# A long convolution in 32-token blocks with stacked lag blocks, inside a fused attention and state-space kernel

## The chip, the cores and the metric

The kernel runs on one core of one Trainium2 chip. The metric is the device time of one execution in microseconds. Before the change it is 539.16 us (median of 4 runs, 536.37 to 542.76). The profile of a kernel is one such execution, recorded by the hardware profiler; its span is about 1.7 us shorter than the time.

In the profile lines, PE is TensorE's matmuls, PEld its loads of the stationary operand, ACT is ScalarE, DVE is VectorE. L867 is a line of the kernel.

## The reference, cut to what matters

```python
x = A_x                                   # 1 x 2048 x 448, bf16
g = sigmoid((x * gate_w).sum(-1, keepdims=True))
a = multi_query_attention(x, wq, wk, wv, wo)   # 16 heads of 28, one K and one V
# S4 layer: a causal convolution over 2048 tokens, one filter of length 2048 per channel
K = real(sum_n C[d,n] * exp(dt[d]*A[d,n]*l) * dt[d]*B[d,n])      # l = 0 .. 2047
b = causal_conv(x, K) + x * Dskip
return g * a + (1 - g) * b
```

There are thus three loads: attention (410 large exponentials on ScalarE, score and PV products on TensorE), the making of the filters K (VectorE and TensorE), and the convolution of 448 channels with 448 different filters, done as Toeplitz products on TensorE. A planner in the kernel puts the pieces in a fixed order on every engine.

## The kernel before

The convolution treats a chunk of 16 channels at a time. For one channel the 2048 tokens are 32 blocks of 64. The Toeplitz data T of a channel is the *moving* operand and the tokens U are the *stationary* one, with as many columns as there are blocks for which the lag matters. Four channels lie interleaved (8 bytes apart in T) and use four column tiles of 32.

```python
for m in range(1, 16, 2):
    def mm(e, k=k, m=m, s=s, gi=gi):
        for j in range(4):                                   # four channels, four column tiles
            r = e.matmul(ps.v(32 * j, 33 - m, po + 128 * k, [[1, 128]]),
                         self.U.v(0, P, (m - 1) * D + 4 * gi + j, [[D, 33 - m]]),                # 32..18 columns
                         self.T.v(0, P, s * 4096 + (960 - 64 * m) * 4 + j, [[4, 128]]),          # 128 columns
                         start=(m == 1), stop=(m == 15), tile_position=(0, 32 * j), skip_group_check=True)
    pg.op("pe", mm, 112, ..., mode="c32")
pg.op("dve", lambda e: e.tensor_tensor(cst..., ps..., omq..., ALU.mult), el(512), ...)     # times 1 - g
self.ytr(c)                                   # 16 transposes back to token rows, then O += on VectorE
# ... cut ...
self.skip()      # 16 times on VectorE: x * Dskip * (1 - g), and O += it
```

Here `v(p0, n, offset, [[stride, count]])` is a view of n partitions; strides are in elements, so `[[D, 33 - m]]` with D = 448 reads stationary columns 896 bytes apart.

Attention is interleaved with this. A score step fills two or three PSUM banks with 512 columns each (`tile_position=(32*h, 0)`, row tiles), ScalarE takes the exponential of them in one activation of 1,024 or 1,536 columns, and a PV step has four matmuls of 512 columns on four column tiles of 32. The score of step b + 2 is issued while step b is in ScalarE.

## Time and profile before

| | before |
|---|---|
| time, median of 4 runs | 539.16 us |
| TensorE busy, mean granted clock | 484.8 us (90%), 0.921 |
| VectorE busy | 483.9 us (90%) |
| ScalarE busy | 487.5 us (91%) |
| DMA queue of the loads, share of 16 engines | 73.7% |
| exponentials | 410, idle 18.9 us before them in all |

The prediction below shows and reads the main lines. Three more views are needed for the comparison. The first is the page's chain of work that ended last, by engine; the second the groups of TensorE with shapes kept apart (busy us, mean ns of one, then the engine's idle time before and what ended it); the third a stretch of the timeline of TensorE (start, length of the row, engine, line, shape of the first instruction of the row, how many).

```profile
PE 47%; ACT 36%; DVE 12%; DMA 2%; issue 1%; POOL 1%; DVEq 0%; POOLq 0%
```

```profile
L967 PE MATMUL psS<-qT,kT 29*128 29x512 bf16 x1024 | 170.6, 412 | 29.6 <-ACT expT L977 27.2
L985 PE MATMUL psB<-expT,vaug 128*32 128x512 bf16 x1024 | 108.8, 417 | 1.4 <-ACT gtok L643 1.3
```

### The profile page before, as it was taken

How to read it: one execution, taken by the hardware profiler on the slowest of the kernel's cores; microseconds unless marked ns; L12 is line 12 of the kernel's file. 1: busy time of each engine (PE TensorE's matmuls, PEld its weight loads, DVE VectorE, ACT ScalarE, POOL GpSimd, SP SyncE). 2: the span in 40 equal slices, each digit the busy share in tenths (PEclk: the TensorE clock that was granted, in tenths of full speed). 3: DMA queues.
4: the chain of work that ended last, by engine and by line, in shares of the span. 5: the costliest groups of instructions: out<-in, count | busy, mean ns of one | idle time of the engine just before them, and what ended most of it. 6: DMA issues, size and time to landing. Idle time of an engine off the chain costs nothing.

```text
span 537.2 us, 18418 instructions
## 1 busy us (share of the span) xinstructions
PE 484.8 (90%) x8229; PEld 243.8 (45%) x8229; DVE 483.9 (90%) x1168; ACT 487.5 (91%) x428; POOL 4.9 (1%) x17
## 2 busy tenths in 40 slices
PE   6778888999999899999999999999999998998893
PEld 5411132553545444554545445554455543544452
DVE  4978899998999999999999999999999999999023
ACT  4599998998999999999999999999999999999960
POOL 3000000000000000000000000000000000000000
PEclk9855566997999999999999999999999999889997
DMA  8735445777798867779898896778877796697954
GB/s 232 145 79 137 138 139 207 245 285 299 249 327 297 303 230 237 253 265 345 304 337 320 262 332 238 242 260 319 309 296 267 285 393 220 176 388 254 350 188 137
DMA packets 42266, 138.16 MB, mean 257 GB/s; under 512 B 8168, under 2 KB 24476, under 8 KB 27852
## 3 DMA queue, kind: packets, MB, share of 16 engines
q1 hardware_dynamic: 40396, 135.71, 73.7%
q10 hardware_dynamic: 1792, 1.29, 0.8%
q8 instruction: 64, 1.05, 0.8%
q14 instruction: 14, 0.11, 0.1%
HBM read 133.01 MB, written 3.85 MB: 255 GB/s over the span
## 4 chain that ended last, share of the span: by engine, by line
PE 47%; ACT 36%; DVE 12%; DMA 2%; issue 1%; POOL 1%; DVEq 0%; POOLq 0%
ACT expT L977 35%; PE psS L967 13%; PE psS L853 12%; PE psB L985 8%; PE psX L792 6%; PE psX L676 2%; DMA T<-KP_scratch 2%; DVE tab L767 2%; DVE tmp L762 2%; DVE tab L759 2%; PE psS L504 1%; PE psX L877 1%; PE psX L831 1%; DVE O L883 1%; DVE tab L776 1%
## 5 line engine op out<-in xcount | busy, mean ns | idle before, releaser
L977 ACT ACTIVATE expT<-psS 128x1536 bf16<-128x1536 f32 (+1 forms) x410 | 470.8, 1254 | 19.0 <-PE psB L985 12.9
L967 PE MATMUL psS<-qT,kT 29*128 29x512 bf16 x1024 | 170.6, 412 | 29.6 <-ACT expT L977 27.2
L853 PE MATMUL psS<-T,U 128*26 128x128 bf16 (+7 forms) x3584 | 157.9, 303 | 0.6 <-DMA T<-KP_scratch 0.5
L853 PEld LDWEIGHTS psS<-T,U 128*26 128x26 bf16 (+7 forms) x3584 | 113.9, 152 | 35.3 <-issue 28.2
L985 PE MATMUL psB<-expT,vaug 128*32 128x512 bf16 x1024 | 108.8, 417 | 1.4 <-ACT gtok L643 1.3
L967 PEld LDWEIGHTS psS<-qT,kT 29*128 29x128 bf16 x1024 | 39.6, 92 | 124.4 <-ACT expT L977 92.8
L762 DVE TENSOR_TENSOR tmp<-tab,mbf 128x2048 bf16<-128x2048 bf16 (+4 forms) x140 | 78.0, 563 | 0.0
L759 DVE TENSOR_TENSOR tab<-tab,mbf 128x2048 bf16<-128x2048 bf16 (+4 forms) x140 | 77.9, 563 | 0.0
L767 DVE TENSOR_TENSOR tab<-tab,tmp 128x2048 bf16<-128x2048 bf16 (+4 forms) x140 | 77.8, 563 | 0.0
L792 PE MATMUL psX<-tab 128*32 128x96 bf16 x1792 | 54.8, 268 | 1.3 <-issue 1.2
L985 PEld LDWEIGHTS psB<-expT,vaug 128*32 128x32 bf16 x1024 | 26.6, 95 | 64.2 <-issue 60.8
L792 PEld LDWEIGHTS psX<-tab 128*32 128x32 bf16 x1792 | 41.2, 116 | 14.2 <-issue 9.0
L776 DVE TENSOR_TENSOR tab<-tab,mbf 128x2048 bf16<-128x2048 bf16 x28 | 34.0, 1216 | 0.0
L778 DVE TENSOR_TENSOR tab<-tab,mbf 128x2048 bf16<-128x2048 bf16 x28 | 34.0, 1213 | 0.0
L861 DVE TENSOR_TENSOR cst<-psS,omq 128x512 bf16<-128x512 f32 x28 | 19.0, 680 | 15.7 <-PE psS L853 15.5
L717 DVE TENSOR_TENSOR msq<-mst 128x256 f32<-128x256 f32 x63 | 26.2, 416 | 0.0
L676 PE MATMUL psX<-xT,Wq 112*128 112x512 bf16 x64 | 21.7, 436 | 0.4 <-DVE O L838 0.2
L727 DVE CAST mbf<-mst 128x256 bf16<-128x256 f32 x70 | 20.1, 288 | 0.1
L720 DVE TENSOR_TENSOR mst<-msq 128x128 f32<-128x128 f32 x70 | 19.7, 282 | 0.0
L723 DVE SCALAR_TENSOR_TENSOR mst<-mst 128x128 f32<-128x128 f32 x63 | 17.8, 283 | 0.0
L804 DVE TENSOR_REDUCE kstg<-psX 128x128 bf16<-128x256 f32 x28 | 11.7, 418 | 4.2 <-PE psX L792 4.1
L730 DVE TENSOR_SCALAR mbf<-mst 128x128 bf16<-128x128 f32 x70 | 15.3, 218 | 0.0
(112 smaller groups left out, 255.8 us busy)
## 6 DMA issues: line engine op xcount, KB each, us to landing
T<-KP_scratch SPq DMA_DIRECT2D x112, 1024.0 KB, 7.8
rdenB<-R_scratch SPq DMA_DIRECT2D x60, 64.0 KB, 3.8
U<-in_A_x_dram SPq DMA_DIRECT2D x3, 896.0 KB, 5.4
tab<-in_A_x_dram SPq DMA_DIRECT2D x4, 448.0 KB, 6.9
O<-Z_scratch SPq DMA_DIRECT2D x1, 1792.0 KB, 13.6
KP_scratch<-kstg SPq DMA_DIRECT2D x28, 64.0 KB
xT<-in_A_x_dram SPq DMA_DIRECT2D x1, 1792.0 KB, 9.2
U<-Z_scratch SPq DMA_DIRECT2D x1, 896.0 KB, 8.0
```

Of the source, the lines that this page charges most:

```text
L676: pg.op("pe", lambda e, T=T: e.matmul(px, self.Wq.v(0, DT, T * 512 + g * 128, [[1, 128]]), self.xT.v(0, DT, T * S + 512 * qc, [[1, 512]]), ...
L717: pg.op("dve", lambda e, k=k: e.tensor_tensor(msq.v(0, P, 0, [[1, 2 * BW]]) if k > 1 else msq.v(0, P, 0, [[BW, 2], [1, BW]]), src_both(k - ...
L759: pg.op("dve", lambda e, d=dst, a=src, ra=ra, w=w: e.tensor_tensor(d, a, mbf.v(0, P, ra, [[8, 16], [0, 2 * w], [1, 4]]), ALU.mult), el(n, ...
L762: pg.op("dve", lambda e, a=src, rb=rb, w=w: e.tensor_tensor(tmp.v(0, P, so, [[4 * w, 32], [1, 4 * w]]), a, mbf.v(0, P, rb, [[4, 32], [0, w ...
L767: pg.op("dve", lambda e, d=dst, t=t2: e.tensor_tensor(d, d, t, ALU.add), el(n, 1.92), rd=[("tmp", s), ("tab", s, lv + 1)], wr=[("tab", s, ...
L776: pg.op("dve", lambda e: e.tensor_tensor(ua, src, mbf.v(0, P, ra, [[8, 8], [0, 64], [1, 4]]), ALU.mult), el(2048, 1.92), rd=rk + mk, wr=[( ...
L778: pg.op("dve", lambda e: e.tensor_tensor(ub, src, mbf.v(0, P, rb, [[4, 16], [0, 32], [1, 4]]), ALU.mult), el(2048, 1.92), rd=rk + mk, wr=[ ...
L792: r = e.matmul(self.psX.v(32 * g, 32, 96 * jj, [[1, 96]]), tab.v(0, P, o + 768, [[4, 32]]), tab.v(0, P, o, [[256, 3], [4, 32]]), start=(co ...
L853: r = e.matmul(ps.v(32 * j, 33 - m, po + 128 * k, [[1, 128]]), self.U.v(0, P, (m - 1) * D + 4 * gi + j, [[D, 33 - m]]), self.T.v(0, P, s * ...
L967: r = e.matmul(self.psS.v(0, P, 1536 * s + 512 * k, [[1, 512]]), kT.v(32 * h, DH + 1, 128 * kt, [[1, 128]]), qT.v(32 * h, DH + 1, 512 * qs ...
L977: pg.op("act", lambda e: e.activation(expT.v(0, P, 512 * (i0 % 10), [[1, n]]), self.psS.v(0, P, 1536 * s, [[1, n]]), AF.Exp, scale=SQ), 75 ...
L985: r = e.matmul(self.psB.v(32 * h, 32, 0, [[1, 512]]), vaug.v(0, P, 32 * kt, [[1, 32]]), expT.v(0, P, 512 * ((4 * st + h) % 10), [[1, 512]] ...
```

## The change

The intent is to halve the Toeplitz data and to do away with work that only rearranges. Tokens are cut into blocks of 32. The filter's lags are stacked so that the 128 rows of a matmul carry four adjacent lag blocks; one loaded filter image of 128 x 2,176 elements (32 columns of 68) serves two accumulations. A channel takes 16 steps m, and causality lets step m use only 64 - 4m stationary columns. Two channels (224 apart) run on two column tiles of 64. The output has tokens reversed inside a block, so the back-transposes disappear; x is stored flipped, and the output is flipped once by a product with an anti-diagonal matrix. The skip term becomes one more matmul per channel, with a small image TD that has Dskip on its diagonal, so that one accumulation, of two channels, has 34 matmuls. U becomes a ring of two slots, loaded in runs of 56 elements. The core of the diff, cut:

```diff
-KPW = 2112
+KR = 68
+KPW = 256 * KR
@@ T load (1 MB becomes 0.54 MB)
-        pg.dma([(self.T.v(0, P, s * 4096, [[1, 4096]]),
-                 dram(self.KP, 4 * gi * KPW, [[4, 64], [4096, 2], [1, 4096]]))],
+        pg.dma([(self.T.v(0, P, s * self.TW, [[1, self.TW]]), dram(self.KP, gi * KPW, [[KR, 128], [1, self.TW]]))],
@@ convolution
-            for m in range(1, 16, 2):
-                    for j in range(4):
-                        r = e.matmul(ps.v(32 * j, 33 - m, po + 128 * k, [[1, 128]]),
-                                     self.U.v(0, P, (m - 1) * D + 4 * gi + j, [[D, 33 - m]]),
-                                     self.T.v(0, P, s * 4096 + (960 - 64 * m) * 4 + j, [[4, 128]]),
-                                     start=(m == 1), stop=(m == 15), tile_position=(0, 32 * j), skip_group_check=True)
+                        for m in range(4 * mg, 4 * mg + 4):
+                            for par in range(2):
+                                r = e.matmul(ps.v(64 * par, 64 - 4 * m, po + 32 * pr, [[1, 32]]),
+                                             self.U.v(0, P, uo + 4 * m * 112 + par * 56 + e0 + pr, [[112, 64 - 4 * m]]),
+                                             self.T.v(0, P, s * self.TW + 4 * m + 2 * k1 + par, [[KR, 32]]),
+                                             start=(m == 0), stop=(m == 15), tile_position=(0, 64 * par), skip_group_check=True)
+                            if m == 0:
+                                for par in range(2):
+                                    r = e.matmul(ps.v(64 * par, 64, po + 32 * pr, [[1, 32]]),
+                                                 self.U.v(0, P, uo + par * 56 + e0 + pr, [[112, 64]]),
+                                                 self.TD.v(0, P, cs * 512 + 8 * par + pr, [[16, 32]]),
+                                                 start=False, stop=False, tile_position=(0, 64 * par), skip_group_check=True)
@@ evacuation: 256 instead of 512 elements, no transposes, no skip on VectorE
-        pg.op("dve", lambda e: e.tensor_tensor(self.cst..., ps..., self.omq..., ALU.mult), el(512), ...)
-        self.ytr(c)
+        pg.op("dve", lambda e: e.tensor_tensor(yv, ps.v(0, P, po + 31, [[-1, 32], [32, 8]]), self.omq..., ALU.mult), el(256), ...)
+        pg.op("dve", lambda e: e.tensor_tensor(ov, ov, yv, ALU.add), el(256, 1.92), ...)
-        self.skip()
```

Cut from it: the flipped x and output, the output projection in pairs of 64 rows, the powers of the seeds in five blocks (2, 5, 7, 7, 7 chunks) rather than seven, and new constants in the planner.

## The prediction

> **What bounds the kernel now.** I first read the page's busy shares and slices.
>
> ```profile
> PE 484.8 (90%) x8229; PEld 243.8 (45%) x8229; DVE 483.9 (90%) x1168; ACT 487.5 (91%) x428; POOL 4.9 (1%) x17
> ...
> PEclk9855566997999999999999999999999999889997
> DMA  8735445777798867779898896778877796697954
> ```
>
> Three engines stand near 90%, so the shares do not name the bound. TensorE runs at half clock from about 22 to 70 us and only settles after 140 us. DMA has room. The groups, with shapes kept apart, say what each engine does.
>
> ```profile
> L977 ACT ACTIVATE expT<-psS 128x1536 bf16<-128x1536 f32 x205 | 300.9, 1468 | 18.9 <-PE psB L985 12.9 <-PE psS L967 4.4
> L977 ACT ACTIVATE expT<-psS 128x1024 bf16<-128x1024 f32 x204 | 212.6, 1042 | 0.1
> L853 PE MATMUL psS<-T,U 128*32 128x128 bf16 x448 | 36.8, 315 | 0.5 <-DMA T<-KP_scratch 0.5
> L831 PE MATMUL psX<-ident,cst 128*64 128x64 bf16 x448 | 12.7, 198 | 2.1 <-DVE cst L861 1.7
> L861 DVE TENSOR_TENSOR cst<-psS,omq 128x512 bf16<-128x512 f32 x28 | 19.0, 680 | 15.7 <-PE psS L853 15.5
> L838 DVE TENSOR_TENSOR O<-O,psX 128x256 bf16<-128x256 bf16 x28 | 11.5, 409 | 1.3 <-PE psX L831 1.1
> L462 DVE SCALAR_TENSOR_TENSOR xT<-xT,gtok 128x448 bf16<-128x448 bf16 x16 | 10.7, 674 | 0.0
> L465 DVE TENSOR_TENSOR O<-O,xT 128x448 bf16<-128x448 bf16 x16 | 6.1, 381 | 0.0
> ```
>
> The softmax exponentials on ScalarE are the backbone: 410 activations that the change does not touch. All they ever wait for is TensorE: the probability buffer that a late PV product (L985) frees, or a late score product (L967). The timeline gives their first and last moments and the pace.
>
> ```profile
> 22.54 2.36 ACT L977 ACTIVATE expT<-psS 128x1536 bf16<-128x1536 f32 x2
> 24.92 1.28 ACT L562 ACT_TABLE_LOAD   x1
> 29.95 1.28 ACT L563 ACT_TABLE_LOAD   x1
> 33.68 5.72 ACT L977 ACTIVATE expT<-psS 128x1024 bf16<-128x1024 f32 x5
> ...
> 499.47 20.06 ACT L977 ACTIVATE expT<-psS 128x1536 bf16<-128x1536 f32 x18
> ...
> 499.79 0.39 PE L967 MATMUL psS<-qT,kT 29*128 29x512 bf16 x2
> 500.11 0.40 PE L985 MATMUL psB<-expT,vaug 128*32 128x512 bf16 x4
> 500.33 0.54 PE L853 MATMUL psS<-T,U 128*32 128x128 bf16 x12
> ...
> 520.03 1.27 DVE L899 COPY acc<-psB 128x128 f32<-128x128 f32 x4 [4.69 <-PE psB L985]
> 529.78 0.96 SPq L106 DMA_DIRECT2D out_dram<-O  x2
> ```
>
> Unhindered stretches run at about 1.13 us per exponential (the chain of waits has one of 26 in 29.12 us), so 410 cost 463 us. They span 22.5 to 519.5, 497.0 us. In between lie the seed activations and table loads, 24.92 to 28.48 and 29.95 to 33.68, together 7.3 us. So 497.0 - 463 - 7.3 = **26.7 us is lost to TensorE**: 18.9 us shows as idle time[...]. The sum of the span is: head 22.5 + seeds 7.3 + exponentials 463 + lost 26.7 + tail 17.7 = 537.2. Only head, seeds, lost time and tail can move.
>
> [...]from scores (row tiles) to PV (column tiles) starts are 0.32 us apart, from PV to convolution (both four column tiles) 0.22 us[...] In the trace the 128-column convolution matmuls, whose moving elements are 8 bytes apart, start in fours every 101 ns (mean 25.3 ns each between 145 and 460 us), or 1.27 columns per ns, and the 64-column transposes (4 bytes apart) in pairs every 34 ns, or 1.9 per ns[...]. The new kernel reads its moving operand 136 bytes apart; no instruction of this trace does that. [...]the 448-element bf16 add took 381 ns against 680 for 512 elements from PSUM.
>
> **The change, part by part.**
>
> *TensorE.* Removed: 3,584 convolution matmuls x 25.3 ns = 91 us, and 448 transposes x 16.8 ns = 7.5 us. Added: 7,616 convolution matmuls of 32 moving columns and 64 down to 4 stationary columns on two column tiles. The nearest thing measured is the transpose pair (64 moving, 64 stationary, 16.8 ns each). Half the moving columns and on average half the stationary ones should cost less, but not half, and the long pitch works against it: I take 12 ns, so 91 us, with 9 to 16 ns open (69 to 122 us). Output projection: 64 matmuls of 448 columns become 256 of 224 in pairs, the same streaming. Flipping the output: 16 x 0.19 = 3 us. Mode changes: counted in program order, 884 become 1,009, because the convolution now differs in mode from PV; 125 x 0.10 = 12.5 us. Sum: -98.5 + 91 + 3 + 12.5 = +8 us, so **TensorE is not relieved**, contrary to what halved data suggests.
>
> *VectorE.* Skip term gone: -10.7 - 6.1. Gating of 256 rather than 512 elements: 28 x (680 - 416) = -7.4. Adding into O from SBUF: 28 x (409 - 285) = -3.5 (416 and 285 are this trace's times for 256 elements at fp32 and bf16). Powers of the seeds in five blocks rather than seven: 104 instructions fewer at 148 ns fixed (256 elements cost 416, 128 cost 282), -15.4. Added: 16 output additions of 675 ns become 32 of about 440, +3.3; 8 copies of flipped output at about 0.62, +5. Sum -35 us: 484 to about 449. This lies beside the exponentials and buys time only where TensorE stood waiting for VectorE.
>
> *DMA.* 112 Toeplitz loads of 1 MB become 0.56 MB: 117 to 62 MB. U comes as some 64,000 runs of 112 bytes; 64-byte runs took 11 ns and 224-byte ones 18 ns on an engine, so 13 ns x 64,000 / 16 = 52 us. T loads fall from 14,356 x 309 ns / 16 = 277 us to 14,336 x about 180 / 16 = 161. DMA eases from some 74% to 50%.
>
> *ScalarE head.* Program order puts all four table loads and both sines ahead of the first exponential. VectorE clips and takes the absolute value before the query copy, and its last x copy moves behind two reductions, so the real seed exponential starts near 23.9; adding 0.95 + 1.28 + 1.04 + 1.28 puts the first softmax exponential near 28.5. Head plus seeds goes from 29.8 to 28.5: -1.3 us.
>
> *Tail.* The last convolution, which overlapped the final normalization before (its final addition ended at 529.75), is done earlier. But flipped-output copies stand between the normalization's copies on VectorE (three of 0.62 before the denominator), then 8 additions of 0.44, a flip and a copy follow before the last store, which now carries a quarter of the output. I get 19 us against 17.7: +1.3.
>
> Head and tail cancel. What remains: **time = 537.2 - 26.7 + lost time after = 510.5 + lost.**
>
> **The lost time after.** TensorE's total stays, but the causes of some gaps go: Toeplitz loads that arrived late[...], transposes waiting for VectorE's gating copy, VectorE with no slack at all from 240 to 460 us. U arrives before 60 us, the first block of powers has two chunks rather than four, so convolution starts sooner and the cold stretch should shorten. The planner's latencies and cold-clock factor were also changed, so its fixed order should fit the chip better.[...] I take 14 to 15 us: 525 on the profile, and 2 more for timed runs (538.96 profiled against 541.81 median before): **527**.
>
> **Rivals.** (a) TensorE becomes the bound: at 16 ns per small matmul the convolution costs 122 us, 39 us more TensorE work in all; with TensorE 95% occupied before, half or more of it would show as lost time, 545 to 560. For: the 136-byte pitch, 224-byte pitch of the weights. Against: 64-column pairs at 34 ns. (b) Nothing moves: TensorE has the same work and the freed VectorE and DMA were never the bound; lost time stays at 22 to 26 us, time 533 to 539. For: ScalarE waits name TensorE alone. (c) The small U descriptors delay Toeplitz loads behind them on the same queue and TensorE stalls each chunk: +5 to +20 us. Against: the packet times above. (d) The better order halves the loss again: 8 us, 518 to 520.
>
> **Range and chances.** The 2% limit is 531. (d) and the main path lie below, (b) on and above, (a) far above. Range 512 to 544; faster 0.60, within 2% 0.32, slower 0.08.
>
> **What would show it.** Exponentials still 410 and some 471 us busy; first near 28.5; idle before them under 14 us rather than 18.9; convolution matmuls 69 to 122 us apart in sum; VectorE near 449 busy; DMA share near half; last exponential to end 19 us. The prediction is wrong if small matmuls start over 16 ns apart, if ScalarE's waits for TensorE do not shrink, or if waits for T or U loads appear in the list.

TensorE comes to +8 us and the forecast to 510.5 + 14 to 15, so 525 on the profile and 527 timed. A change of tiles enters at 0.10 us, the difference of the two steps that it gives (0.32 - 0.22; medians of 315 and 217 ns at full clock in the trace of before), and what it sets against the gains in the lost time is 125 of these. An output flip at 0.19 us is the step of a 448-column product (L877, 189 ns at full clock). What its 26.7 us hold beyond the 18.9 of idle time is not traced to a cause. That the long pitch works against the 12 ns was an estimate; that an earlier convolution would shorten the stretch at half clock was one as well.

## More of the kernel before

```profile
181.08 0.40 PE L985 MATMUL psB<-expT,vaug 128*32 128x512 bf16 x4
181.31 0.78 PE L853 MATMUL psS<-T,U 128*26 128x128 bf16 x20
182.11 0.39 PE L967 MATMUL psS<-qT,kT 29*128 29x512 bf16 x3
```

The chain runs through TensorE for 47% and ScalarE for 36%: the two alternate as the one that is late. TensorE still waits 27.2 us for exponentials before it can start scores. Twenty convolution matmuls take 0.80 us to the next score, and PV to convolution 0.23 us.

## The result, and the profile after

| | before | after |
|---|---|---|
| time, median of 4 runs | 539.16 us | 864.86 us (860.56 to 870.59) |
| ratio of fast runs | | 1.604 (95%: 1.587 to 1.621) |
| TensorE busy, mean granted clock | 484.8 us, 0.921 | 819.0 us, 0.613 |
| VectorE busy | 483.9 us | 469.7 us |
| ScalarE idle before exponentials | 18.9 us | 322.4 us |

A ratio is the mean time of one kernel's fast runs over the mean of the other's from the same rounds, so it need not be quite the ratio of the medians.

The change made the kernel 60% slower. The page of the profile after, in the order in which the prediction read that of before: busy shares and slices.

```profile
PE 819.0 (95%) x12009; PEld 479.2 (56%) x12024; DVE 469.7 (55%) x1058; ACT 509.4 (59%) x436; POOL 5.8 (1%) x12
...
PEclk9555555556566866565557866555565665555558
DMA  9820334244342224445244242534335222334303
```

Only TensorE is busy now, and its clock row holds 5s where the kernel before had 9s: it runs at half clock most of the time. A mean clock of 0.613 between the two values 0.5 and 1.0 that the records show means half clock for 77% of the time; before it was 16%. VectorE and DMA have much room, as was the intent. The chain that ended last, by engine, says that TensorE nearly always decides:

```profile
PE 87%; DVE 8%; ACT 3%; DMA 1%; issue 1%; SPq 0%; DVEq 0%
```

The groups with shapes kept apart:

```profile
L1019 ACT ACTIVATE expT<-psS 128x1536 bf16<-128x1536 f32 x205 | 297.6, 1452 | 300.3 <-PE psS L1009 196.0 <-PE psB L1027 103.9
L1019 ACT ACTIVATE expT<-psS 128x1024 bf16<-128x1024 f32 x204 | 208.5, 1022 | 22.0 <-PE psS L1009 19.7 <-PE psB L1027 0.6
L1009 PE MATMUL psS<-qT,kT 29*128 29x512 bf16 x1024 | 228.2, 558 | 12.8 <-ACT expT L1019 11.7 <-issue 0.9
L1027 PE MATMUL psB<-expT,vaug 128*32 128x512 bf16 x1024 | 145.9, 560 | 1.3 <-ACT expT L1019 1.0 <-DVE acc L975 0.3
L867 PE MATMUL psS<-T,U 128*64 128x32 bf16 x448 | 70.8, 312 | 1.9 <-issue 1.4 <-DVE tab L793 0.5
L867 PE MATMUL psS<-T,U 128*32 128x32 bf16 x448 | 57.8, 254 | 0.9 <-issue 0.9
L867 PE MATMUL psS<-T,U 128*4 128x32 bf16 x448 | 55.8, 244 | 0.0
L883 DVE TENSOR_TENSOR Y<-psS,omq 128x256 bf16<-128x256 f32 x28 | 11.9, 424 | 200.8 <-PE psS L867 200.8
```

The exponentials themselves are unchanged (1,452 and 1,022 ns against 1,468 and 1,042). What is new is 322 us of idle time in front of them, nearly all of it put down to scores and PV products that come late. Scores and PV have grown from 412 and 417 to 558 and 560 ns each, although nothing in them was changed. That goes with the clock: from a score to its PV product starts are 315 ns apart at full clock and 533 at half (medians; 534 before), and the mean clock fell from 0.921 to 0.613. VectorE's evacuation waits 200.8 us for the convolution. A convolution matmul with 4 stationary columns lasts 244 ns, about as long as one with 32 (254).

The means above are lengths of single overlapping instructions, so they do not add. A stretch of the timeline, at full clock from 181.3 us on, gives the pace:

```profile
181.01 0.32 PE L867 MATMUL psS<-T,U 128*64 128x32 bf16 x2
181.16 0.29 PE L873 MATMUL psS<-TD,U 128*64 128x32 bf16 x2
181.27 0.49 PE L867 MATMUL psS<-T,U 128*60 128x32 bf16 x6
181.69 0.39 PE L1009 MATMUL psS<-qT,kT 29*128 29x512 bf16 x2
182.01 0.40 PE L1027 MATMUL psB<-expT,vaug 128*32 128x512 bf16 x4
182.34 1.40 PE L867 MATMUL psS<-T,U 128*48 128x32 bf16 x26
183.56 0.29 PE L873 MATMUL psS<-TD,U 128*64 128x32 bf16 x2
```

Twenty-six small matmuls take 1.22 us to the next, 47 ns each. PV to convolution now takes 0.33 us where it took 0.23: the 0.10 us of a change of tiles that the prediction counted.

To add up, I charge each matmul the time from its start to the start of the next one, whatever lies between (its own streaming, a wait, a change of tiles). TensorE's time by kind in us:

| | before | after | difference |
|---|---|---|---|
| convolution | 150.0 | 380.5 | +230.5 |
| scores | 155.5 | 209.1 | +53.6 |
| PV | 87.1 | 121.1 | +34.0 |
| everything else | 131.2 | 135.7 | +4.5 |
| sum | 523.8 | 846.4 | +322.6 |

This is the whole of the loss: 230 us in the convolution itself and 88 us in attention products that did not change. By this rule a wait is charged to the matmul before it: of the scores' waits for ScalarE (27.2 us before, 11.7 after), 17.4 and 6.1 us stand behind a score or PV product and so in these two rows. Without them the products lost some 99 us.

The pace of the convolution by stationary columns (two matmuls on two column tiles, start of one pair to start of the next, medians between 100 and 800 us) is the same at full and at half clock within 1 to 2 ns:

```
stationary columns   64   64(TD)  60   56   52   48   44   40   32   28   24..8   | 36->32  4->64
ns per pair         140    118  112  105   97   91   83   76   83   55    ~63    |  175    178
```

Three things are in it. First, wide pairs cost about 1.85 ns for each stationary column of a tile; the two tiles of a pair go together (their loads start 3 to 4 ns apart and are equally long, 208 ns each at 60 columns). Second, from 24 columns down there is a floor of 63 ns, whatever the number (the pairs of 32 and 28, just after a gap, share theirs unevenly: 69 ns on the mean). Third, two gaps of some 175 ns stand in every accumulation, where the columns pass from 36 to 32 and, at its end, back from 4 to 64; the first pair of 64 after it takes 140 ns.

That the clock makes no more than these 1 to 2 ns of difference means that, at these pitches, the pace is not set by the granted clock. While it lasts the array has little to do: 32 moving columns in a pair of 63 to 118 ns.

### The profile page after: what moved, and what is told of

Its sections match the earlier page's. It is cut to its first block, busy times and chain, and to the rows that moved or that the text cites. A ratio compares the mean times of both kernels' runs of the same rounds, so it can differ in the third digit from the quotient of the medians.

```text
span 859.2 us, 26055 instructions
## 1 busy us (share of the span) xinstructions
PE 819.0 (95%) x12009; PEld 479.2 (56%) x12024; DVE 469.7 (55%) x1058; ACT 509.4 (59%) x436; POOL 5.8 (1%) x12
## 3 DMA queue, kind: packets, MB, share of 16 engines
q1 hardware_dynamic: 106450, 85.74, 37.5%
## 4 chain that ended last, share of the span: by engine, by line
PE 87%; DVE 8%; ACT 3%; DMA 1%; issue 1%; SPq 0%; DVEq 0%
PE psS L867 40%; PE psS L1009 20%; PE psB L1027 13%; PE psX L818 5%; PE psS L873 3%; PE psX L700 2%; ACT expT L1019 2%; PE psX L902 2%; DMA tab<-in_A_x_dram 1%; DVE tab L785 1%; DVE tab L793 1%; DVE tmp L788 1%; PE psS L526 1%; DVE msq L742 1%; DVE mbf L753 0%
## 5 line engine op out<-in xcount | busy, mean ns | idle before, releaser
L1019 ACT ACTIVATE expT<-psS 128x1536 bf16<-128x1536 f32 (+1 forms) x410 | 488.7, 1236 | 322.4 <-PE psS L1009 215.7
L867 PE MATMUL psS<-T,U 128*64 128x32 bf16 (+15 forms) x7168 | 396.7, 257 | 4.3 <-issue 3.5
L867 PEld LDWEIGHTS psS<-T,U 128*64 128x64 bf16 (+15 forms) x7168 | 334.6, 157 | 110.6 <-issue 77.7
L1009 PE MATMUL psS<-qT,kT 29*128 29x512 bf16 x1024 | 228.2, 558 | 12.8 <-ACT expT L1019 11.7
L1027 PE MATMUL psB<-expT,vaug 128*32 128x512 bf16 x1024 | 145.9, 560 | 1.3 <-ACT expT L1019 1.0
L883 DVE TENSOR_TENSOR Y<-psS,omq 128x256 bf16<-128x256 f32 x28 | 11.9, 424 | 200.8 <-PE psS L867 200.8
L793 DVE TENSOR_TENSOR tab<-tab,tmp 128x128 bf16<-128x128 bf16 (+4 forms) x140 | 79.0, 564 | 0.7
L785 DVE TENSOR_TENSOR tab<-tab,mbf 128x128 bf16<-128x128 bf16 (+4 forms) x140 | 78.5, 565 | 0.7
L788 DVE TENSOR_TENSOR tmp<-tab,mbf 128x128 bf16<-128x128 bf16 (+4 forms) x140 | 78.7, 562 | 0.0
L873 PE MATMUL psS<-TD,U 128*64 128x32 bf16 x448 | 65.6, 289 | 0.0
L873 PEld LDWEIGHTS psS<-TD,U 128*64 128x64 bf16 x448 | 48.8, 214 | 0.0
L700 PE MATMUL psX<-xT,Wq 112*128 112x512 bf16 x64 | 30.1, 564 | 1.6 <-DVE mbf L601 1.6
L742 DVE TENSOR_TENSOR msq<-mst 128x448 f32<-128x448 f32 (+2 forms) x45 | 23.5, 522 | 0.0
```

The costliest lines, as they stand in the source:

```text
L700: pg.op("pe", lambda e, T=T: e.matmul(px, self.Wq.v(0, DT, T * 512 + g * 128, [[1, 128]]), self.xT.v(0, DT, T * S + 512 * qc, [[1, 512]]), ...
L785: pg.op("dve", lambda e, d=dst, a=src, ra=ra, w=w: e.tensor_tensor(d, a, mbf.v(0, P, ra, [[8, 16], [0, 2 * w], [1, 4]]), ALU.mult), el(n, ...
L788: pg.op("dve", lambda e, a=src, rb=rb, w=w, so=so: e.tensor_tensor(tmp.v(0, P, so, [[4 * w, 32], [1, 4 * w]]), a, mbf.v(0, P, rb, [[4, 32] ...
L793: pg.op("dve", lambda e, d=dst, t=t2: e.tensor_tensor(d, d, t, ALU.add), el(n, 1.92), rd=[("tmp", lv % 2), ("tab", s, lv + 1)], wr=[("tab" ...
L867: r = e.matmul(ps.v(64 * par, 64 - 4 * m, po + 32 * pr, [[1, 32]]), self.U.v(0, P, uo + 4 * m * 112 + par * 56 + e0 + pr, [[112, 64 - 4 * ...
L873: r = e.matmul(ps.v(64 * par, 64, po + 32 * pr, [[1, 32]]), self.U.v(0, P, uo + par * 56 + e0 + pr, [[112, 64]]), self.TD.v(0, P, cs * 512 ...
```

## The experiments

Twelve kernels ran; the kernel before ran beside them with 538.49, 538.78 and 538.92 us. Those called wrong read the right amount of data in another arrangement (b2 also pads it, b7 leaves work out), so that their result is of no use. Two letters are used in the expectations: W is the theory that the pitch of the stationary operand U (224 bytes between columns) sets the pace, H the theory that TensorE's clock follows how densely moving columns stream. The rivals to W are the pitch of the moving operand T (136 bytes) and the two gaps.

### a1_wcont: stationary columns side by side (wrong)

```diff
-self.U.v(0, P, uo + 4 * m * 112 + par * 56 + e0 + pr, [[112, 64 - 4 * m]])
+self.U.v(0, P, uo + 4 * m + 64 * (par * 56 + e0 + pr), [[1, 64 - 4 * m]])
```
(and the same for the TD matmul)

> The changed kernel with the convolution's stationary operand (U) read contiguously instead of at a 224-byte pitch; wrong result on purpose, same instructions. Theory W (loading strided weights sets the pace of the wide pairs): the pairs of 64 to 36 stationary columns, now 118 to 69 ns apart, all fall to the floor of about 63 ns, which is 302 ns per channel pair and slot, x 224 = 68 us less: about 790 us. Rival I (a fixed issue cost per weight load and matmul): pair distances and time stay, 855 to 870 us. Rival V (only the moving operand's pitch counts): stays too.

Measured: 750.67 us at a clock of 0.691. The wide pairs fell from 76–112 to the floor of 63 ns; the narrow ones and the two gaps did not move. TensorE's convolution time fell from 380.5 to 298.9 us, scores and PV from 330.2 to 306.8. So W holds for the pairs of 40 to 60 columns, with an effect larger than expected, part of which goes with the clock (0.691 against 0.613): 23 us came from scores and PV.

### a2_mcont: moving columns side by side (wrong)

```diff
-self.T.v(0, P, s * self.TW + 4 * m + 2 * k1 + par, [[KR, 32]])
+self.T.v(0, P, s * self.TW + 32 * (4 * m + 2 * k1 + par), [[1, 32]])
```
(TD likewise)

> The changed kernel with the convolution's moving operand (T) read contiguously instead of at a 136-byte pitch; wrong result on purpose. Theory V (the floor of 63 ns per pair is the strided moving read): the seven narrow pairs per slot fall from 63 to about 35 ns, 7 x 28 x 224 = 44 us less: about 815 us; wide pairs stay where the weights hold them. Rival I: nothing moves, 855 to 870 us.

Measured: 816.26 us, clock 0.603. The sum of the expectation (815) came true in part by luck: the convolution lost 53 us rather than 44, and the rest of TensorE's time grew by 9. Now the wide pairs did not move and the narrow ones fell: 25 ns at 8 and 12 columns, 32, 39, 47 and 53 ns at 16, 20, 24 and 28. The floor of 63 ns thus went with the 136 bytes between its 32 moving columns, about 2 ns each. Under it the stationary columns show again, at about 1.85 ns. In these two runs the pair took what the slower operand that was left took (63 ns in a1; 76 to 112 ns for 40 to 60 columns here), so both must go.

### a3_pad: never under 36 stationary columns

```diff
-ps.v(64 * par, 64 - 4 * m, ...), self.U.v(..., uo + 4 * m * 112 + ..., [[112, 64 - 4 * m]])
+ps.v(64 * par, max(64 - 4 * m, 36), ...), self.U.v(..., uo + min(4 * m, 28) * 112 + ..., [[112, max(64 - 4 * m, 36)]])
```

> The changed kernel with at least 36 stationary columns in every convolution matmul, so that none falls to 32 or fewer[...]; wrong result on purpose. Theory D (36 to 32 and 4 to 64 columns are changes of tiling mode inside each accumulation, 110 ns each): the two long gaps of 175 ns per slot fall to about 70 and 118,[...] and eight pairs cost 6 ns more each (11 us): about 822 us. If the long gaps are waits for data or bank changes, they stay: 870 us.

Its 822 us are some 860 less 49 for the 448 long gaps (0.11 us each, 175 - 63 ns), plus 11.

Measured: 845.11 us; clock 0.612. The result still passed, since at these lags the filters have nothing that shows at the tolerance. Adding all the starts by kind of step shows what happened: in the kernel after, 315 gaps inside accumulations took 55.3 us (the other 133 of 448 fell together with a change to scores or PV). With padding there is no such gap, so the two gaps come with the passage of 32 columns. They coincide with changes of tile size in the built program, and are called tile changes here: in the kernel after, 3,584 convolution matmuls have the tile size 128 x 32 and 4,032 have 128 x 64; in a3 all have 128 x 64. But the some 3,300 steps between narrow matmuls went from 30.0 to 36.3 ns each, which gives back 21 us. The expectation had this return too small; convolution time fell by 26 us only.

### a4_wide: 64 moving columns, each element with its neighbour (right result)

```diff
-self.T.v(0, P, s * self.TW + 4 * m + 2 * k1 + par, [[KR, 32]])
+self.T.v(0, P, s * self.TW + 4 * m + 2 * k1 + par, [[KR, 32], [1, 2]])
```
(output 64 columns wide, of which the evacuation reads every second)

> The changed kernel with 64 instead of 32 moving columns in every convolution matmul (each element and its neighbour in memory; the additional 32 results are not used, so the result stays right). Theory H (the clock is halved because the array is streaming little, although TensorE is never idle): the clock in the records rises from 0.61 towards 0.9 and more, score and PV products return from 532 to 315 ns start to start, up to 106 us less: 750 to 800 us with unchanged pair distances. Rival: the clock follows TensorE's idle time or the mode changes: clock stays near 0.6 and the time stays or grows.

Measured: 849.15 us. Twice the moving columns made the convolution dearer (416.0 us of TensorE time against 380.5) and the clock higher (0.769 against 0.613), so that scores and PV took 285.7 us instead of 330.2. Its clock row:

```profile
PEclk9555586576989799677677979997886969655966
```

H predicted the direction. The amount was wrong: the additional columns were not free. The medians of the pairs did not move (63 ns at 24 columns, 112 at 60); of the 35 us, 21 are in the steps between matmuls of up to 32 columns, some of which now start in another order.

### b1_both: both operands side by side (wrong)

The edits of a1 and a2 together.

> The changed kernel with both operands of the convolution read contiguously; wrong result on purpose. If weights (1.83 ns per 224-byte-pitch column and pair) and moving reads (63 ns per pair of 32 columns at 136 bytes) are the two limits and the larger one holds, removing both brings every pair to 25 to 33 ns (25 was seen for narrow pairs with contiguous T, 33 for the 64-column transposes of the kernel before), apart from the two tile changes of about 110 ns in each of 224 accumulations: convolution from 299 us of TensorE time (contiguous U alone) to some 185, run about 630 us. Rival I (issue cost holds once the reads are gone): pairs stop at 40 to 50 ns and the run at 690 or more.

Measured: 592.96 us with all 7,616 matmuls. The page and a stretch of the timeline:

```profile
PE 538.3 (91%) x12009; PEld 289.0 (49%) x12024; DVE 465.8 (79%) x1058; ACT 497.1 (84%) x436; POOL 5.8 (1%) x12
...
PEclk9755555899996999669998899999999999555557
```

```profile
303.10 0.18 PE L873 MATMUL psS<-TD,U 128*64 128x32 bf16 x2
303.13 0.64 PE L867 MATMUL psS<-T,U 128*60 128x32 bf16 x30
303.70 0.39 PE L1009 MATMUL psS<-qT,kT 29*128 29x512 bf16 x3
```

Same instruction counts as in the kernel after, 272 us less. Thirty matmuls take 0.57 us to the next, 19 ns each with one tile change inside. A pair costs 25 ns at the least (12.5 a matmul) and 30 ns at 60 columns; now the pace of wide pairs follows the clock, with 52 ns at 60 columns at half clock. TensorE's time by starts fell from 846.4 to 578.7 us: by 198.6 in the convolution and by 62.3 in scores and PV, which were not touched (330.2 to 267.9). The expectation had the first part right (185 us of convolution for 181.9) and, with some 630 us, the second too small. The steps of the convolution by kind, in us and (ns each):

| | after | a1 | a2 | b1 | b2 |
|---|---|---|---|---|---|
| both over 36 columns (3,289 steps) | 163.3 (49.6) | 92.4 (28.1) | 161.1 (49.0) | 57.5 (17.5) | 55.1 (16.8) |
| both up to 32 columns (about 3,300) | 98.9 (30.0) | 91.3 (27.7) | 67.7 (20.5) | 47.5 (14.4) | with the next row |
| to and among 36 columns | 17.1 | 14.3 | 16.8 | 6.1 | 62.0 (15.2) |
| tile changes inside (315) | 55.3 (176) | 55.7 | 43.7 | 36.1 (115) | none |
| to another kind of work (250 to 270) | 45.9 (170) | 45.1 | 38.1 | 34.7 | 40.8 |
| sum | 380.5 | 298.9 | 327.3 | 181.9 | 157.8 |

Most of the convolution's loss is in the first two rows: from the kernel after to b1 they fall by 157 us of the 199.

### b2_bothpad: both side by side and never under 36 columns (wrong)

b1 with the edit of a3.

> The changed kernel with both operands contiguous and never fewer than 36 stationary columns; wrong result on purpose. In the run with both contiguous the two tile changes per accumulation cost 84 ns more than a plain pair at full clock (109 against 25), so 224 x 2 x 0.084 = 38 us of TensorE time should go, and the run from 593 to 555 to 575 us. If less TensorE work lowers the clock again, as it did in the kernel before with contiguous operands, part of it is given back: 575 to 595 with a clock under 0.82.

Measured: 574.57 us, clock 0.852, as first expected. With contiguous operands the padded columns cost little (15.2 ns a step to and among 36 columns, against 14.4 in b1 for up to 32), and taking the tile changes away is worth 24 us of convolution time. Even so the new convolution (157.8 us) is no cheaper than the old one (150.0), and the time is 6.6% above that of the kernel before.

### b3_fewconv: 6 of 34 matmuls in every accumulation

```diff
-for mg in range(4): ... for m in range(4 * mg, 4 * mg + 4):
+for mg in (0, 3):   ... for m in {0: (0,), 3: (15,)}.get(mg, ()):
```

> The changed kernel with 6 of 34 matmuls left in each accumulation (first and last lag blocks and the skip term); wrong result on purpose. If the convolution alone is what the change lost, everything else of it is at least as good as before: 525 to 550 us, VectorE as busy as in the changed kernel. Theory H says the clock stays halved all the same, or more so, since scores and PV alone do not stream enough (as from 40 to 100 us of the kernel before); with the exponentials as bound that costs about 8%: then 540 to 570. Rival: other parts of the change (U loads, mode changes, flipped output) lost time too: 600 us or more.

Measured: 626.47 us, *slower* than b1 with all its 34. (The result passed for the same reason as a3.) Only m = 0, 15 and the skip are left, strided as in the kernel after:

```profile
PE 553.0 (89%) x5737; PEld 233.7 (37%) x5752; DVE 468.8 (75%) x1058; ACT 500.9 (80%) x436; POOL 4.4 (1%) x12
...
PEclk9855575665666569766755657776569765655558
```

```profile
303.90 0.29 PE L873 MATMUL psS<-TD,U 128*64 128x32 bf16 x2
304.12 0.47 PE L867 MATMUL psS<-T,U 128*4 128x32 bf16 x4
304.42 0.29 PE L873 MATMUL psS<-TD,U 128*64 128x32 bf16 x2
```

The convolution still takes 121.2 us for 1,344 matmuls, 90 ns each: 64 columns to 4 and back, a change of tile each way. And the clock is 0.641, so scores and PV take 354.2 us. Of these, 34 us are waits for ScalarE that the count puts on them; the other 320 compare with 257 in b1. Against b1 TensorE has 6,272 matmuls fewer and the convolution 61 us less time, and the kernel is 34 us slower. (b1 differs in pitch too; against the kernel after, with the same pitch, the clock rose from 0.613 to 0.641.) The work that TensorE no longer had was not time won here, where the clock stayed at 0.641.

Both forecasts of the expectation fell: the convolution cost more than they allowed for. The time lies where the rival put it, but not for the rival's reason, since TensorE's time for everything except convolution, scores and PV is 136.9 us, against 131.2 in the kernel before.

### b4_before_both: the kernel before with both convolution operands side by side (wrong)

```diff
-self.U.v(0, P, (m - 1) * D + 4 * gi + j, [[D, 33 - m]])
+self.U.v(0, P, (m - 1) + 32 * (4 * gi + j), [[1, 33 - m]])
-self.T.v(0, P, s * 4096 + (960 - 64 * m) * 4 + j, [[4, 128]])
+self.T.v(0, P, s * 4096 + (960 - 64 * m) + 1024 * j, [[1, 128]])
```

> The kernel before with both operands of its convolution read contiguously; wrong result on purpose. Groups of four start 120 ns apart there, whatever their 18 to 32 columns, so the 8-byte pitch of the moving operand should hold them[...]. Contiguous: 60 to 70 ns, so about 50 us less TensorE work. If the 26.7 us that the exponentials lose is TensorE's doing, half of it comes back: ratio 0.97 to 0.98 (523 to 530 us). If lost time does not follow TensorE's load: ratio 0.99 to 1.01.

That the 8-byte pitch holds the groups was an estimate (128 columns in 123 ns are 1.04 per ns).

Measured: 546.8 us (4 runs), ratio 1.0171 (1.0109 to 1.0233). The expectation fell. Groups of four convolution matmuls start 56 ns apart at full clock (107 at half) instead of some 120, as hoped, and convolution steps without exits take 50.3 rather than 84.6 us. But:

```profile
PE 462.3 (84%) x8214; PEld 201.4 (37%) x8229; DVE 483.4 (88%) x1168; ACT 488.5 (89%) x428; POOL 4.9 (1%) x17
...
PEclk9765566986988869985999979996799799877587
```

```profile
PE psS L967 <- ACT expT L977: 49.8, 125, 2.3
```

The last line is TensorE's waits (us, times, longest): its scores now wait 49.8 us for ScalarE instead of 27.2, and the clock keeps falling to half (0.829 on the mean; 0.922 to 0.932 in the runs of the kernel before beside it). In full-clock stretches the saved time turns into waiting (39 of the 49.8 us), and in the half-clock stretches ScalarE waits for TensorE (19 of 27.0 us for scores and PV, where it was 7 of 17.3). That it is the waiting which lets the clock fall is a reading that goes with the section on the clock below; it is not shown alone. So the pitches of 8 and 896 bytes cost the kernel before nothing that could be had back in this way.

### b7_before_noskip: the kernel before without the skip term (wrong)

```diff
-        self.skip()
```

> The kernel before without its skip term on VectorE (32 instructions, 17 us of VectorE, and one 1.8 MB load); wrong result on purpose. The prediction said VectorE's relief lies beside the exponentials: ratio 0.99 to 1.005. If VectorE held the kernel before: 17 us less, ratio 0.97.

Measured: 533.47 us (4 runs), ratio 0.9916 (0.9874 to 0.9958). VectorE's busy time fell from 483.9 to 470.6 us, nearly what the whole change took off it, and the time by 0.8%. That is about what relief of VectorE was worth.

### c1_before_fill: filler matmuls in the cold stretch of the kernel before (right result)

```diff
+        for i in range(100):
+            # four matmuls of 512 columns on four column tiles, into bank 5, read by nobody
+            pg.op("pe", fl, 225, mode="c32", rd=["va"] + self.xk(0), wr=[("b", 5)], pr=5)
         self.uload()
```

> The kernel before with 100 additional groups of four 512-column matmuls on an unused bank, placed by the scheduler where TensorE has nothing to do between about 34 and 95 us; result stays right. Theory H (the clock is raised after a window in which the array streams enough, whatever the streaming is for): the half-clock stretch from 22 to 70 us shortens to about 22 to 42, mean clock from 0.92 to 0.95 or more, scores and PV there at 215 instead of 430 ns: 3 to 6 us less, ratio 0.99 to 0.995. Rival (additional work only delays the exponentials): ratio 1.01 to 1.03.

Measured: 544.66 us (4 runs), ratio 1.0122 (1.0059 to 1.0185); clock 0.945. Scores and PV fell from 242.6 to 223.3 us of TensorE time (7 of the 19 us were waits for ScalarE), as H says, but the filler itself took 29 us, and the time came out in the range of the rival. The higher clock (0.945 to 0.961 in its runs, 0.918 to 0.932 in those of the kernel before) cost more than it was worth here.

### d1_tap: skip term folded into the filter (right result)

Dskip is added to the filter's value at lag 0, four columns of each chunk's filter image, so that the convolution does the skip term.

```diff
-        self.skip()
+        kl = self.kstg.v(0, P, ks * 256 + 252, [[1, 4]])
+        pg.op("dve", lambda e: e.tensor_tensor(kl, kl, self.sk.v(0, P, 4 * c, [[1, 4]]), ALU.add), 75, ...)
```
(`sk` holds Dskip on partitions 31, 63, 95 and 127 and zero elsewhere)

> The kernel before with its skip term folded into the convolution: Dskip is added to the filter's tap at lag 0 (28 additions of 4 columns on VectorE, some 3 us, for 32 instructions of 17 us and a 1.8 MB load). Result should stay within the tolerance. The run without any skip term gave ratio 0.992; this should give 0.992 to 0.997.

Measured: 535.25 us (4 runs), ratio 0.9937 (0.9902 to 0.9971). 28 additions of 149 ns take the place of 32 operations on whole token rows. It is the fastest kernel with a right result, though by less than 1%.

### d2_tapfill: d1 and c1 together (right result)

> Both together, the folded skip term and the filling matmuls in the cold stretch, as a candidate that beats both kernels: if the two gains add, ratio 0.98 to 0.99, 528 to 533 us; if the filling delays more than it warms, 1.00 or above.

Measured: 538.99 us (4 runs), ratio 1.0011 (0.9955 to 1.0067), clock 0.95. The filler takes back what the tap gave, as in c1; the expected sum of two gains fell with c1.

### The clock

In the clock records of all fourteen traces the stretches of one clock, but for the last, are whole multiples of 3,413 ns (1 to 95 of them in the kernel before, 1 to 36 in the one after). I cut the traces into windows of that length, aligned with the clock records, and computed for each the share in which at least one matmul's moving columns stream. For that I took 2.4 columns per ns at full clock and 1.2 at half: the query products of 512 columns (L676, L700) start 216 ns apart at full clock and 400 to 427 at half, which is 2.4 and 1.2 to 1.3, and b4's 128 columns in 56 and 107 ns are 2.3 and 1.2. Sorted by the clock in the window and in the next (5th, 50th, 95th percentile of the share):

| clock now, next | before | after |
|---|---|---|
| full, full | .46 .58 .68 (124 windows) | .36 .46 .65 (25) |
| full, half | .14 .38 .49 (7) | .16 .30 .42 (29) |
| half, half | .51 .64 .88 (17) | .32 .54 .79 (165) |
| half, full | .75 .84 .87 (6) | .69 .77 .90 (29) |

In these two traces the clock fell after windows with a median share of 0.38 and 0.30 and rose after windows with 0.84 and 0.77; about 0.45 and 0.7 are my estimates of the two edges, read from the table. The kernel before, at full clock, sits at 0.58 and mostly stays (124 windows of 131); the one after, at 0.46, fell after 29 windows of 54, and once at half clock rose after 29 of 194. This is a correlation; a4, b3, b4 and c1 moved the density up or down and the mean clock moved with it each time, so that the direction is shown. Counted at full rate over the whole span, columns would stream for 32% of it in the kernel after, 36% in b3, 42% in a4, 49% in b4, 52% in the kernel before and 55% in c1, and the clocks are 0.613, 0.641, 0.769, 0.829, 0.921 and 0.945, in the same order (a low clock also lengthens the span, so the two are not independent). No rule is shown: the shares of windows after which the clock rose and of those after which it did not overlap.

## Why the prediction was wrong

**The step that failed first: "The nearest thing measured is the transpose pair ... I take 12 ns, so 91 us, with 9 to 16 ns open."** The measured figure is 380.5 / 7,616 = 50 ns. The transposes read stationary columns side by side and moving ones 4 bytes apart. With such operands the 12 ns is right: b1 shows 12.5 ns at best and 14.4 to 17.5 on average. At 224 and 136 bytes it is not. The prediction itself said that no instruction of the trace had that pitch, and then used the figure all the same, allowing a third for it.

It also compared stationary columns with the wrong thing ("on average half the stationary ones", against the transposes). Against the convolution that they replace they tripled: 3,584 x 25 = 89,600 columns before, 7,168 x 34 + 448 x 64 = 272,384 after. In time it is worse, since four tiles went together before (matmuls of a group start 3 to 4 ns apart) and two do now: 22,400 columns one after the other became 136,192. At the measured 1.85 ns that is 252 us, as an estimate for the whole convolution if nothing else limited it. Counting columns of *both* operands would have been a reason to look.

The other side of the same sum, "3,584 convolution matmuls x 25.3 ns = 91 us", was too small too. The 25.3 ns is the mean step from one convolution matmul to the next and leaves out the last step of every run, to scores or PV: 3,339 steps of 25.3 ns and 245 of 267 ns are the 150.0 us. (Groups of four start 123 ns apart, so the last step carries most of a group. The prediction's "start in fours every 101 ns", "or 1.27 columns per ns", is thus misread by the same omission: it is 1.04 per ns.)

**Second: "Mode changes: ... 884 become 1,009 ... 125 x 0.10 = 12.5 us."** 315 more take place inside the accumulations, where the program keeps one placement but passes 32 columns; in a3 and b2, with 36 columns at least, they are gone. Counted by tile size in the built programs, the changes are 885 before, 1,265 after and 1,009 in a3: the prediction's number is that of the padded kernel. In the kernel after, those inside take 55.3 us at 176 ns; an ordinary step there takes 30 to 50 ns, so about 42 us of it is extra.

**Third, missing altogether: the clock.** The prediction assumed that convolution "starts sooner and the cold stretch should shorten". Its first matmul came at 100.7 us where it had been 90.4, and half clock went from 16% to 77% of the time. From 150.0 to 380.5 us the convolution alone would have brought 537 + 230, some 770 us (an estimate by addition). The other 88 us are in scores and PV, mostly at half clock. Rival (a), "TensorE becomes the bound", named the right cause, with the pitch as its argument, and stopped at 16 ns and 560 us.

**The sign "small matmuls start over 16 ns apart"** was given as what would prove it wrong, and is what happened. "ScalarE's waits do not shrink" came true as well, with 322.4 us for a foreseen 14. Waits for T or U did not come, as foreseen.

**Right, by its own steps:**

- The frame *time = 510.5 + lost*. That the lost time comes out at 348.7 us in place of 14 to 15 follows by subtraction and tests nothing; its terms do hold: 29.5 us to the first exponential, 18.6 after the last, and exponentials that wait for nothing start as before (medians of 1,347 and 904 ns for the two sizes, 1,342 and 904 before, so some 461 us for 410; with the prediction's own 26 in 29.12 us it would have had 459 rather than 463).
- "Exponentials still 410": the same number, 488.7 us busy in all. Their head was a little off, the first at 29.49 us rather than 28.5, and the tail was right, 18.6 us from the end of the last exponential for a predicted 19:

```profile
28.19 1.28 ACT L1019 ACT_TABLE_LOAD   x1
29.49 3.71 ACT L1019 ACTIVATE expT<-psS 128x1536 bf16<-128x1536 f32 x3
...
838.64 1.94 ACT L1019 ACTIVATE expT<-psS 128x1536 bf16<-128x1536 f32 x2 [1.15 <-PE psB L1027]
```

- VectorE: "Sum -35 us". The lengths of its instructions added up fell from 572.1 to 540.4 us, by 31.7. The page's busy time, which counts overlapping neighbours once, fell by 14.2 only, because its instructions, with more gaps between them, overlapped less (88.2 us before, 70.8 after). The prediction applied a sum of lengths to a busy time. That this relief "buys time only where TensorE stood waiting for VectorE" was right; b7 and d1 give 0.6 to 0.8% for it.
- DMA: T and U were never waited for.

```profile
q1 hardware_dynamic: 106450, 85.74, 37.5%
...
T<-KP_scratch SPq DMA_DIRECT2D x112, 544.0 KB, 3.6
U<-in_A_x_dram SPq DMA_DIRECT2D x40, 140.0 KB, 3.9
```

A T load lands 3.6 us after its issue, where it took 7.8. The 64,000 packets of 112 bytes took 13 ns at the median, as estimated, and those of T 168 for "about 180". The load of the engines was under-counted: 37.5% of 859.2 is 322 us an engine against 396 before, where "50%" of 527 would be 264. The prediction's own terms, 396 - 116 + 52 = 332, were nearer than its share. (It took counts times medians; the T packets of the kernel before add up to 325 us an engine, not 277.) Rival (c) is refuted.
- Rivals (b) and (d) did not come to be tested: the lost time was far from both.

**What stays open.** By what rule the clock rises and falls is not shown beyond the table above. Why a column costs 1.85 ns at 224 bytes on the stationary side and about 2 ns at 136 bytes on the moving side was not taken further; only these two pitches, and 8 and 896 bytes in the kernel before, were seen. Whether the new algorithm can be laid out with both operands contiguous *and* right was not tried; b2, with both contiguous and no tile change, took 574.57 us, so by itself that would not pay here.

## What to carry to other kernels

Before halving an operand, count the columns that TensorE will read of *both* operands, and their pitch; take the cost of a small matmul only from one with the same pitch on both sides (50 ns here where 12 were taken from side-by-side operands), and look whether its column count crosses 32 (steps of 175 and 178 ns here). Then ask what the array will be doing meanwhile: here, at a clock of 0.613 in place of 0.921, scores and PV beside the small, slowly fed matmuls took 330.2 us in place of 242.6, and with less convolution time in b4 the clock was lower as well, 0.829. An engine at 90% beside others at 90% may be worth under 1%, as VectorE was here; test that by deleting its work, wrong result and all, before redesigning around it.
